# q and k loaded with twelve tokens of one head per partition, and transposed in 64 by 64 pieces

## The chip, the core and the metric

The kernel runs on one core of a Trainium2 chip. The core has five engines that run side by side, each through its own instructions in order: TensorE (PE in the profile; its weight loads are shown apart as PEld), VectorE (DVE), ScalarE (ACT), GpSimd (POOL) and SyncE (SP). Data comes from HBM into SBUF by DMA, through 16 DMA engines that all queues share. TensorE reads SBUF and writes PSUM, and VectorE and ScalarE take results out of PSUM. SBUF and PSUM have 128 partitions each.

The metric is the device time of one execution in microseconds (us). The time before is 165.16 us, the median of three runs (163.99, 165.16 and 166.20).

## The reference

The program is an attention that looks at few chunks of keys, and a soft mixture of experts (MoE) over its result. Sizes: 4 batches, 8 heads, 768 tokens, head dimension 64; chunks of 32 keys, of which 6 are chosen per query; 8 experts with 4 slots each, model width 512, hidden width 1024.

```
k_min, k_max = min and max of k over each chunk of 32 keys
ub     = sum_d max(q * k_min, q * k_max)       # bound of a query's score with a chunk
ub     = where(chunk not after the query's chunk, ub, -1e9)
chosen = the 6 chunks with the largest ub, per query
scores = q @ k.T / sqrt(64), -1e9 where the chunk isn't chosen or the key is later
attn   = softmax(scores) @ v                   # 4 x 8 x 768 x 64

x      = attn as 3072 x 512
logits = x @ phi                               # 3072 x 32
d      = softmax of logits over the tokens;  slot_in = d.T @ x
slot_out[e] = relu(slot_in[e] @ w1[e]) @ w2[e]
out    = softmax of logits over the slots @ slot_out
```

## The kernel before

The attention is worked through in 16 pairs of heads: pair i holds two heads of one batch, and each batch has four pairs. For a product over the head dimension, q and k must lie in SBUF with that dimension on the partitions. The kernel keeps them as `kT` and `qT`, 128 partitions by 768 tokens in bf16: partitions 0 to 63 are the 64 dimensions of the pair's first head, 64 to 127 those of the second.

The path from HBM to `kT` (and to `qT` alike) has three steps.

- `load` (L141 to L147) issues one DMA from GpSimd for one pair and one tensor. It converts from f32 to bf16. In `k_in` (or `q_in`), partition p holds tokens 6p to 6p + 5 of the first head and then the same tokens of the second: two runs per partition, each 6 x 64 f32 values or 1.5 KB in HBM.
- `transposes` (L203 to L213) makes 12 transposing matmuls. For each of the six token places g and each head h, 128 partitions by 64 columns of `k_in` are the stationary operand, and the 128 by 128 identity moves through. The result, 64 dimensions by 128 tokens, goes to the partition half h of the PSUM tile `tr_ps`, at place g. Both heads' pieces thus stand in the same PSUM tile, one above the other.
- `evac_T` (L215 to L222) is one ScalarE copy of `tr_ps` into `kT`, which puts the tokens into their order: token 6p + g is read from place g, column p.

`kT` is then read by VectorE for the chunks' minima and maxima (`kmin`, `kmax`), and by TensorE for the scores. `qT` is split by VectorE into its negative and positive parts (`qsplit`, tile `qpn`), which `ubound` multiplies with the chunks' bounds (tile `ub_ps`). `select` takes the six largest on VectorE, `ns_transposes` brings the choice to the scores' layout, and `scores` (L294 to L313) adds the product of q and k (L301) and the mask of the choice (L311) in PSUM. `expo` takes the exponential on ScalarE (L325), GpSimd masks the blocks on the diagonal (L335), `pv` multiplies with v (L353, tile `at_ps`), and `normalise` divides on VectorE. The result is transposed (`x_transposes`, L375) and goes into the MoE.

The order of work is written out by hand, engine by engine. In step i of the loop over pairs, the scores and exponentials of pair i run in six groups; between them stand the bounds and the choice of pair i + 1, the transposes of pair i + 2, the products with v of pair i - 1, and the normalisation and transposes of pair i - 2. On TensorE, the k transposes follow the bounds (`ubound(i + 1)`) and precede `pv(i - 1, [0, 1, 2])` and the scores of groups 2 and 3; the q transposes follow `pv(i - 1, [3])` and precede the scores of group 4. On ScalarE, the copy to `kT` stands between the exponentials of groups 1 and 2, the copy to `qT` between those of groups 3 and 4. The scores go through two PSUM tiles of two banks each, one bank per head. The tile `tr_ps` shares two one-bank buffers (`p_tp`) with the other small results of TensorE.

Loads are issued from GpSimd, whose instructions run in order with the masks: k and q of pair i + 4 in step i, v of pair i + 2, and one or two of the 16 weight blocks of the experts (1 MB each in SBUF, `w_sb`). The loop starts at step 1. Ahead of it, pairs 0 and 1 are prepared with filler matmuls on TensorE (`warm`, L201) between their transposes, step 0 is written out by itself with the transposes of pair 2, and the loads of pairs 0 to 4 are issued. After the loop come the last pair, the experts, and the output.

Of the kernel before, what the change touches and what calls it, by code (L numbers as in the profile page):

```python
# [11 lines left out]
BF16 = mybir.dt.bfloat16  # L12
# [8 lines left out]
NQT = 6  # L21
P = 128
S = 768
D = 64
# [36 lines left out]
def kernel(  # L61
# [10 lines left out]
    nc = tc.nc  # L72
# [6 lines left out]
    SPE = NS // E  # L79
    NDG, NFG = Dm // P, F // P  # L80
    EARLY = 14
    LAST = NPAIR - 1

    ctx.enter_context(tc.manual_schedule())
# [5 lines left out]
    p_tp = ctx.enter_context(tc.tile_pool(name="p_tp", bufs=2, space=PSUM))  # L90
# [4 lines left out]
    ident = static.tile([P, P], BF16, name="ident")  # L95
# [9 lines left out]
    w1p = w_ctx.enter_context(tc.tile_pool(name="w1p", bufs=1, side="right"))  # L105
    for i in range(EARLY):
        w_sb.append((w1p if i < E else static).tile([P, NDG * F], BF16, name=f"w_sb{i}"))
# [21 lines left out]
    inp = l_ctx.enter_context(tc.tile_pool(name="inp", bufs=3, side="right"))  # L129
# [11 lines left out]
    def load(i, nm):  # L141

        b, j = divmod(i, NPB)
        t = inp.tile([P, 2, NQT * D], BF16, name=nm + "_in", tag=nm + "_in")
        src = {"k": k, "q": q}[nm][b, 2 * j:2 * j + 2]
        nc.gpsimd.dma_start(out=t, in_=src.rearrange("h (p g) d -> p h (g d)", p=P))  # L146
        st[nm, i] = t  # L147

    def load_v(i):
        b, j = divmod(i, NPB)  # L150
        nc.gpsimd.dma_start(  # L151
            out=v_t[i % NV][:, :, :, :D],
            in_=v[b, 2 * j:2 * j + 2].rearrange("h (g p) d -> p h g d", p=P),
        )


    nc.vector.memset(ones_sq, 1.0)
    load(0, "k")
    load(0, "q")
    make_identity(nc, ident)  # L160
    for t in (squad, caus, qgrp, headsel, ns_t[0], ns_t[1], c_pad):
# [6 lines left out]
    for j in range(4):  # L168
# [3 lines left out]
        out=squad, in_=squad, compare_op=ALU.not_equal, fill=NEG, base=0,  # L172
# [3 lines left out]
        out=squad, in_=squad, compare_op=ALU.not_equal, fill=-1.0, base=-NCHUNK,  # L176
        pattern=[[-CH, 2], [-64, 2], [0, NCHUNK]], channel_multiplier=1,
    )
    load(1, "k")
    load(1, "q")  # L180
    nc.gpsimd.affine_select(
        out=qgrp, in_=qgrp, compare_op=ALU.not_equal, fill=1.0, base=0,
# [3 lines left out]
        out=caus[:4], in_=caus[:4], compare_op=ALU.is_ge, fill=NEG, base=0,  # L186
# [15 lines left out]

    def transposes(i, nm):  # L203

        ps = p_tp.tile([P, NQT, P], BF16, name="tr_ps", tag="tp")
        src = st.pop((nm, i))
        for g in range(NQT):
            for h in range(2):
                nc.tensor.matmul(  # L209
                    ps[h * 64:(h + 1) * 64, g, :], lhsT=src[:, h, g * D:(g + 1) * D], rhs=ident,  # L210
                    is_transpose=True,
                )
        st[nm + "ps", i] = ps  # L213

    def evac_T(i, nm):  # L215

        t = tp3.tile([P, S], BF16, name=nm + "T", tag=nm + "T")
        nc.scalar.copy(  # L218
            t.rearrange("d (p g) -> d p g", g=NQT),
            st.pop((nm + "ps", i)).rearrange("d g p -> d p g"),  # L220
        )
        st[nm + "T", i] = t  # L222
# [71 lines left out]
    def scores(i, g):  # L294
        ps = p_sc.tile([P, 2, 512], F32, name="sc_ps", tag="sc")
        kT, qT, nsT = st["kT", i], st["qT", i], st["nsT", i]
        for kg, q0, w, c in (GROUPS_LAST if i == LAST else GROUPS)[g]:
            qs = slice(kg * P + q0, kg * P + q0 + w)
# [19 lines left out]
    def expo(i, g, masked=True):  # L318
        pieces = (GROUPS_LAST if i == LAST else GROUPS)[g]
        w = sum(x[2] for x in pieces)  # L320
        if w == 512:
            e = ep.tile([P, 2, 512], BF16, name="e_sb", tag="e_sb")
        else:
            e = ep3.tile([P, 2, 384], BF16, name="e3_sb", tag="e3_sb")
        nc.scalar.activation(e[:, :, :w], st.pop(("scps", i, g))[:, :, :w], func=ACT.Exp, scale=scale)  # L325

        st["e", i, g] = e
        if masked:
            mask(i, g)

    def mask(i, g):
        e = st["e", i, g]
        for kg, q0, _, c in (GROUPS_LAST if i == LAST else GROUPS)[g]:
            if q0 == 0:
# [5 lines left out]
    def pv(i, ts):  # L340
        if i == LAST and ts[0] == 0:
            st["at", i] = p_tp.tile([P, 2, 3 * (D + 1)], F32, name="at_ps", tag="tp")
        elif i == LAST and ts[0] == 3:
            st["at", i] = p_sc.tile([P, 2, 512], F32, name="at_ps", tag="sc")
        elif ts[0] == 0:
            st["at", i] = p_at.tile([P, 2, 512], F32, name="at_ps", tag="at")
        at, tb = st["at", i], 3 if i == LAST and ts[0] > 2 else 0
        for t in ts:
            for h in range(2):
                o = at[:, h, (t - tb) * (D + 1):(t - tb + 1) * (D + 1)]  # L350
                for kg in range(t + 1):
                    g, c = (BLOCK_LAST if i == LAST else BLOCK)[(kg, t)]
                    nc.tensor.matmul(  # L353
                        o, lhsT=st["e", i, g][:, h, c:c + P], rhs=v_t[i % NV][:, h, kg, :],
                        start=(kg == 0), stop=(kg == t),
                    )
# [163 lines left out]
    def have(i):  # L520
        return 0 <= i < NPAIR
# [10 lines left out]
    def weights(i):  # L532
        nonlocal nw
        for _ in range(wplan.get(i, 0)):
            load_w(nw)
            nw += 1

    warm(9)
    transposes(0, "k")
    evac_T(0, "k")  # L540
    kmin(0)
    kmax(0)
    warm(3)
    transposes(0, "q")
    evac_T(0, "q")
    qsplit(0)
    warm(2)
    transposes(1, "k")
    evac_T(1, "k")
    warm(2)  # L550
    ubound(0)
# [39 lines left out]
    for i in range(1, NPAIR):  # L591
        slots = have(i - 3) and (i - 3) % NPB == NPB - 1
        if i >= EARLY:
            wt = ctx.enter_context(tc.tile_pool(name=f"wt{i}", bufs=1))
# [47 lines left out]
        if have(i + 2):  # L642
            load_v(i + 2)
        if i < EARLY:
            weights(i)
# [77 lines left out]
    def cinv(n):  # L723
# [5 lines left out]
        bc, lhsT=mneg.broadcast_to([NS, P]), rhs=identf[:NS, :NS], start=True, stop=True,  # L729
# [159 lines left out]
    for m in range(1, NM):  # L889
        o_sb = op.tile([P, 2, Dm], F32, name="o_sb", tag="o_sb")  # L890
        for x, scaled in enumerate((scaled_act, scaled_dve)):
            tag = ("sc", "tp", "tp", "sc", "at")[n % 5]
# [38 lines left out]
```

## Time and profile before

| | |
|---|---|
| time, median of three runs | 165.16 us |
| the profiled execution's own time | 164.61 us |
| its span, first to last instruction | 162.9 us |
| TensorE busy | 140.9 us, 86% of the span |
| VectorE busy | 123.3 us, 76% |
| ScalarE busy | 122.3 us, 75% |
| GpSimd busy | 103.2 us, 63% |
| mean granted TensorE clock | 0.953 |
| read from HBM | 52.49 MB |

The profile is that of one execution, and its times count from the start of the span. Matmuls are pipelined: a matmul's shown duration reaches from its start to its end, and the next one starts long before that end, so what a matmul costs is read from the distance between starts. A row of the timeline joins instructions of one line that follow one another; its two numbers are the start of the first and the time to the end of the last. In a group's row, the busy time and the mean duration in ns are followed by the idle time of the engine just before the group's instructions, and by what ended most of it. The chain of waits is followed back from the last instruction: at each step to what released it, or to the instruction before it on its engine.

### The profile page before, as it was taken

How to read it: one execution, taken by the hardware profiler on the slowest of the kernel's cores; microseconds unless marked ns; L12 is line 12 of the kernel's file. 1: busy time of each engine (PE TensorE's matmuls, PEld its weight loads, DVE VectorE, ACT ScalarE, POOL GpSimd, SP SyncE). 2: the span in 40 equal slices, each digit the busy share in tenths (PEclk: the TensorE clock that was granted, in tenths of full speed). 3: DMA queues.
4: the chain of work that ended last, by engine and by line, in shares of the span. 5: the costliest groups of instructions: out<-in, count | busy, mean ns of one | idle time of the engine just before them, and what ended most of it. 6: DMA issues, size and time to landing. Idle time of an engine off the chain costs nothing.

```text
span 162.9 us, 5890 instructions
## 1 busy us (share of the span) xinstructions
PE 140.9 (86%) x2417; PEld 91.6 (56%) x2417; DVE 123.3 (76%) x434; ACT 122.3 (75%) x168; POOL 103.2 (63%) x203
## 2 busy tenths in 40 slices
PE   7796779999999999999999899998989899986600
PEld 2253456767767686676768567676857544442100
DVE  4466989999999999999997999898555632177620
ACT  3758879999999898999989799996986122075520
POOL 6988759989889498978959897859845400000000
PEclk9999999999999999999999999999999959999555
DMA  3999999999999999999999999999999999229996
GB/s 43 149 148 159 208 179 127 173 197 202 202 202 203 202 206 180 207 198 183 214 191 211 197 208 195 212 214 197 210 199 214 215 215 211 59 82 406 404 404 255
DMA packets 40603, 32.92 MB, mean 202 GB/s; under 512 B 26368, under 2 KB 34816, under 8 KB 40576
## 3 DMA queue, kind: packets, MB, share of 16 engines
q0 software_dynamic: 38416, 26.25, 109.2%
q1 hardware_dynamic: 2160, 6.29, 9.9%
q8 instruction: 19, 0.31, 0.7%
q14 instruction: 8, 0.07, 0.1%
HBM read 52.49 MB, written 6.29 MB: 361 GB/s over the span
## 4 chain that ended last, share of the span: by engine, by line
PE 49%; ACT 17%; DVE 11%; DMA 8%; issue 6%; POOL 4%; POOLq 0%; ACTq 0%; DVEq 0%
ACT e_sb L325 11%; PE sc_ps L301 9%; PE at_ps L353 8%; PE sc_ps L311 6%; DMA out_dram<-o_sb 5%; PE tr_ps L209 5%; PE xT_ps L375 4%; ACT qT L218 3%; PE h_ps L790 3%; DMA k_in<-in_k_dram 3%; PE ub_ps L260 2%; PE so_ps L824 2%; DVE x_sb L366 2%; PE ub_ps L253 1%; DVE mx L272 1%
## 5 line engine op out<-in xcount | busy, mean ns | idle before, releaser
L325 ACT ACTIVATE e_sb<-sc_ps 128x1024 bf16<-128x1024 f32 (+1 forms) x96 | 83.2, 917 | 7.8 <-PE sc_ps L311 7.2
L335 POOL TENSOR_SCALAR_AFFINE_SELECT e_sb<-e_sb 128x256 bf16<-128x256 bf16 x96 | 38.5, 418 | 16.1 <-ACT e_sb L325 15.6
L301 PE MATMUL sc_ps<-qT,kT 64*128 64x384 bf16 (+3 forms) x258 | 36.8, 305 | 2.5 <-ACT e_sb L325 1.6
L311 PE MATMUL sc_ps<-nsT,smask 64*128 64x384 bf16 (+2 forms) x294 | 38.1, 284 | 0.1
L353 PE MATMUL at_ps<-v_t,e_sb 128*128 128x65 bf16 x672 | 29.8, 194 | 1.7 <-DVE x_sb L366 1.3
L353 PEld LDWEIGHTS <-e_sb 128*128 128x128 bf16 x672 | 25.6, 98 | 4.0 <-issue 2.6
L301 PEld LDWEIGHTS <-kT 64*128 64x128 bf16 x258 | 13.9, 93 | 10.6 <-issue 5.3
L272 DVE MAX8 mx<-ub_ps 128x8 f32<-128x8 f32 (+1 forms) x192 | 16.8, 162 | 3.7 <-PE ub_ps L260 2.8
L311 PEld LDWEIGHTS <-smask 64*128 64x128 bf16 x294 | 14.9, 94 | 3.9 <-issue 0.6
L151 POOL DMA_DIRECT2D v_t<-in_v_dram x16 | 16.6, 1038 | 0.6 <-PE ns_ps L283 0.5
L227 DVE TENSOR_REDUCE mm<-kT 128x24 bf16<-128x768 bf16 x16 | 15.1, 944 | 2.2 <-ACT kT L218 2.2
L366 DVE TENSOR_TENSOR x_sb<-at_ps,inv 128x768 bf16<-128x768 f32 (+1 forms) x17 | 15.5, 910 | 0.6
L233 DVE TENSOR_REDUCE mm<-kT 128x24 bf16<-128x768 bf16 x16 | 15.1, 943 | 0.0
L218 ACT COPY qT<-tr_ps 128x768 bf16<-128x768 bf16 x16 | 12.8, 800 | 2.3 <-PE tr_ps L209 2.3
L218 ACT COPY kT<-tr_ps 128x768 bf16<-128x768 bf16 x16 | 12.8, 802 | 1.0 <-PE tr_ps L209 1.0
L146 POOL DMA_DIRECT2D k_in<-in_k_dram x16 | 11.8, 735 | 1.1 <-POOLq L915 0.8
L146 POOL DMA_DIRECT2D q_in<-in_q_dram x16 | 11.5, 716 | 0.0
L139 POOL DMA_DIRECT2D w_sb<-in_moe_w_dram x16 | 11.4, 712 | 0.0
L386 DVE COPY xT_sb<-xT_ps 128x768 bf16<-128x768 bf16 (+1 forms) x15 | 8.0, 537 | 2.6 <-PE xT_ps L375 2.6
L894 PE MATMUL o_ps<-so_all,cT_all 128*128 128x512 bf16 x22 | 7.5, 428 | 2.5 <-ACT o_sb L856 2.2
L247 DVE TENSOR_SCALAR qpn<-qT 128x768 bf16<-128x768 bf16 x15 | 9.2, 610 | 0.0
L209 PE MATMUL tr_ps<-ident,k_in 128*64 128x128 bf16 x192 | 8.4, 223 | 0.6 <-DMA k_in<-in_k_dram 0.5
(137 smaller groups left out, 206.3 us busy)
## 6 DMA issues: line engine op xcount, KB each, us to landing
w_sb<-in_moe_w_dram POOLq DMA_DIRECT2D x16, 1024.0 KB, 12.6
out_dram<-o_sb SPq DMA_DIRECT2D x10, 512.0 KB, 4.9
k_in<-in_k_dram POOLq DMA_DIRECT2D x16, 192.0 KB, 6.3
q_in<-in_q_dram POOLq DMA_DIRECT2D x16, 192.0 KB, 6.9
v_t<-in_v_dram POOLq DMA_DIRECT2D x16, 192.0 KB, 7.7
out_dram<-o_sb SPq DMA_DIRECT2D x2, 256.0 KB, 4.1
out_dram<-first SPq DMA_DIRECT2D x2, 128.0 KB, 2.0
out_dram<-first SPq DMA_DIRECT2D x1, 256.0 KB, 2.1
```

What stands on the lines that cost most here:

```text
L146: nc.gpsimd.dma_start(out=t, in_=src.rearrange("h (p g) d -> p h (g d)", p=P))
L151: nc.gpsimd.dma_start(out=v_t[i % NV][:, :, :, :D], in_=v[b, 2 * j:2 * j + 2].rearrange("h (g p) d -> p h g d", p=P),)
L209: nc.tensor.matmul(ps[h * 64:(h + 1) * 64, g, :], lhsT=src[:, h, g * D:(g + 1) * D], rhs=ident, is_transpose=True,)
L218: nc.scalar.copy(t.rearrange("d (p g) -> d p g", g=NQT), st.pop((nm + "ps", i)).rearrange("d g p -> d p g"),)
L227: nc.vector.tensor_reduce(mm[:, 0, 0, :], kT, axis=AX.X, op=ALU.min)
L272: nc.vector.max(mx[:, a, :], ub[:, a, :max(8, 4 * t + 4)])
L301: nc.tensor.matmul(ps[:, h, c:c + w], lhsT=kT[r, kg * P:(kg + 1) * P], rhs=qT[r, qs], start=True, stop=False,)
L311: nc.tensor.matmul(ps[:, h, c + (f - t0) * P:c + (l - t0) * P], lhsT=smask[r, x, kg].rearrange("p a b -> p (a b)"), rhs=nsT[r, (f - x * NJ ...
L325: nc.scalar.activation(e[:, :, :w], st.pop(("scps", i, g))[:, :, :w], func=ACT.Exp, scale=scale)
L335: nc.gpsimd.affine_select(out=e[:, :, c:c + P], in_=e[:, :, c:c + P], compare_op=ALU.is_ge, fill=0.0, base=0, pattern=[[0, 2], [1, P]], ch ...
L353: nc.tensor.matmul(o, lhsT=st["e", i, g][:, h, c:c + P], rhs=v_t[i % NV][:, h, kg, :], start=(kg == 0), stop=(kg == t),)
L366: nc.vector.tensor_tensor(st["x", b][:, t0:t1, 2 * j:2 * j + 2, :].rearrange("p t h d -> p h t d"), at[:, :, :, :D], inv.broadcast_to([P, ...
```

## The change

`load` gives each partition twelve consecutive tokens of one head: partition 64h + p holds tokens 12p to 12p + 11 of head h, one run of 12 x 64 f32 values or 3 KB in HBM. `transposes` works on pieces of 64 partitions by 64 columns, with the matching 64 by 64 part of the identity: 24 matmuls for a pair and a tensor, whose results fill the same 768 columns of `tr_ps` as 12 places of 64. The pieces of the first head use partitions 0 to 63 of SBUF and of PSUM, those of the second 64 to 127. `evac_T` reads token 12p + g from place g, column p. `kT` and `qT` hold the same as before.

```diff
+    NT2 = 2 * NQT
...
-        t = inp.tile([P, 2, NQT * D], BF16, name=nm + "_in", tag=nm + "_in")
+        t = inp.tile([P, NT2 * D], BF16, name=nm + "_in", tag=nm + "_in")
         src = {"k": k, "q": q}[nm][b, 2 * j:2 * j + 2]
-        nc.gpsimd.dma_start(out=t, in_=src.rearrange("h (p g) d -> p h (g d)", p=P))
+        nc.gpsimd.dma_start(out=t, in_=src.rearrange("h (p g) d -> (h p) (g d)", g=NT2))
...
-        ps = p_tp.tile([P, NQT, P], BF16, name="tr_ps", tag="tp")
+        ps = p_tp.tile([P, NT2, 64], BF16, name="tr_ps", tag="tp")
         src = st.pop((nm, i))
-        for g in range(NQT):
+        for g in range(NT2):
             for h in range(2):
+                r = slice(h * 64, (h + 1) * 64)
                 nc.tensor.matmul(
-                    ps[h * 64:(h + 1) * 64, g, :], lhsT=src[:, h, g * D:(g + 1) * D], rhs=ident,
-                    is_transpose=True,
+                    ps[r, g, :], lhsT=src[r, g * D:(g + 1) * D], rhs=ident[r, r], is_transpose=True,
                 )
...
-            t.rearrange("d (p g) -> d p g", g=NQT),
+            t.rearrange("d (p g) -> d p g", g=NT2),
```

## The prediction

> **What bounds the kernel now.** I read the totals by line first, to see what the transposes are worth at all.
>
> ```profile
> PEclk9999999999999999999999999999999959999555
> ...
> L218 ACT COPY kT<-tr_ps 128x768 bf16<-128x768 bf16 x16 | 12.8, 802 | 1.0 <-PE tr_ps L209 1.0
> ...
> L209 PE MATMUL tr_ps<-ident,k_in 128*64 128x128 bf16 x192 | 8.4, 223 | 0.6 <-DMA k_in<-in_k_dram 0.5
> ```
>
> The k transposes keep TensorE busy for 8.4 us, those of q for as long, and the granted clock is full while they run: every slice up to the 32nd shows a 9. Whether they set the end is read from one steady pair of heads: first TensorE alone, then ScalarE alone.
>
> ```profile
> 48.02 0.53 PE L209 MATMUL tr_ps<-ident,k_in 128*64 128x128 bf16 x12
> 48.48 0.55 PE L353 MATMUL at_ps<-v_t,e_sb 128*128 128x65 bf16 x12
> 48.96 0.34 PE L301 MATMUL sc_ps<-qT,kT 64*128 64x384 bf16 x2
> 49.14 0.33 PE L311 MATMUL sc_ps<-nsT,smask 64*128 64x384 bf16 x2
> 49.30 0.33 PE L301 MATMUL sc_ps<-qT,kT 64*128 64x384 bf16 x2
> 49.46 0.33 PE L311 MATMUL sc_ps<-nsT,smask 64*128 64x384 bf16 x2
> 49.72 0.51 PE L375 MATMUL xT_ps<-ident,x_sb 128*128 128x128 bf16 x6
> 50.07 0.41 PE L353 MATMUL at_ps<-v_t,e_sb 128*128 128x65 bf16 x8
> 50.41 0.53 PE L209 MATMUL tr_ps<-ident,q_in 128*64 128x128 bf16 x12
> ```
> ```profile
> 48.72 0.81 ACT L218 COPY kT<-tr_ps 128x768 bf16<-128x768 bf16 x1
> 49.56 1.51 ACT L325 ACTIVATE e_sb<-sc_ps 128x768 bf16<-128x768 f32 x2
> 50.98 0.80 ACT L218 COPY qT<-tr_ps 128x768 bf16<-128x768 bf16 x1
> 51.67 1.03 ACT L325 ACTIVATE e_sb<-sc_ps 128x1024 bf16<-128x1024 f32 x1
> ```
>
> ScalarE is nearly gapless, yet TensorE leads it here. The copy of qT starts at 50.98 and the next exponential already at 51.67, 0.69 later. The copy of kT starts at 48.72, and the exponential after it only at 49.56, 0.84 later: 0.15 us of waiting, for scores that end at 49.14 + 0.33 = 49.47 and stand behind the k transposes and the products at L353. So a longer k transpose is paid in full. For q the last piece ends at 50.41 + 0.53 = 50.94, and the exponentials leave ScalarE free at about 49.56 + 1.51 - 0.10 = 50.97: the slack is 0.03 us. The chain of waits says the same:
>
> ```profile
> 48.09 0.46 PE tr_ps L209 x12
> ...
> 50.48 0.46 PE tr_ps L209 x12
> ...
> 52.78 0.59 PE lg_ps L395 x24
> ```
>
> Both sets lie on it. Fourteen pairs of heads (2 to 15) are transposed between the scores of earlier pairs, so 28 sets count; those of pairs 0 and 1 stand in the start, between filler matmuls.
>
> **What a set costs now.** A set of 12 takes 48.48 - 48.02 = 0.46 us, start to the start of what follows. To split it I cut the same spot finer:
>
> ```profile
> 48.02 0.14 PEld L209 LDWEIGHTS <-k_in 128*64 128x64 bf16 x4
> 48.02 0.25 PE L209 MATMUL tr_ps<-ident,k_in 128*64 128x128 bf16 x2
> ```
> ```profile
> 48.02 0.30 PE L209 MATMUL tr_ps<-ident,k_in 128*64 128x128 bf16 x4
> ```
>
> Two pieces together last 0.25 us, hardly more than one (0.22 to 0.24): the two heads, which write upper and lower halves of PSUM, run side by side. Four last 0.30, so the second couple starts about 0.08 after the first; twelve last 0.53, so the sixth starts about 0.53 - 0.22 = 0.31 after it, and a couple costs (0.31 - 0.08) / 4 = 0.057. That is the price of 128 columns: at L375 six such matmuls, one by one, last 0.51, (0.51 - 0.22) / 5 = 0.058 each. The weight loads are covered. Price follows columns: couples of 384 wide follow one another every 49.30 - 49.14 = 0.16, which is 0.053 per 128. The rest, 0.46 - 0.31 = 0.15, is the last couple's own 0.055 and a change-over of about 0.10 to the next array shape.
>
> **The change, part by part.** *Transposes.* 24 pieces of 64 rows by 64 columns in place of 12 of 128 by 128, 12 couples in place of 6. If couples still run side by side and cost by width, one costs 0.027 to 0.029. The second then starts 0.08 - 0.028 = 0.052 after the first, ten more make 0.29, and the end is 0.15 - 0.028 = 0.12: 0.46 to 0.47 against 0.46. I take +0.01 per set, times 28: **+0.3 us**. Half the columns, twice the couples: nothing is won or lost. The shapes before and after the set stay others than its own, so the change-overs stay two.
>
> No row shows a 64 by 64 piece, so bounds are needed. Below, 0.0: a tile cannot pass 64 columns faster than 384 go by at L301. Above, pieces that go singly at a full transposing matmul's price, L375: 23 x 0.058 + 0.15 = 1.48, +1.0 per set or +28 us. I take the couples' price, because L209 itself shows couples writing one PSUM tile (768 bf16 values, 1.5 KB a partition) in the same instant, and L301 shows upper and lower rows at work together.
>
> That tile is also where a rule speaks against the change. The Trainium skill, TensorEngine Tiling (Array Packing), Restrictions and Gotchas, says that different row tiles cannot access one PSUM bank at the same time. The two scores at L301 go to different banks, so no run here shows row tiles sharing one. By that rule the pieces would go singly, the second rival below; without it the sum stays +0.3.
>
> *Copies out of PSUM.* Same 128x768, each run of the inner loop 12 long rather than 6. The nearest row with no stride at all is the one copy that ScalarE makes at L386:
>
> ```profile
> 125.34 0.80 ACT L386 COPY xT_sb<-xT_ps 128x768 bf16<-128x768 bf16 x1 [0.52 <-PE xT_ps L375]
> ```
>
> 0.80 like L218, so stride costs nothing: 0.
>
> *Loads.* Same bytes in half the packets.
>
> ```profile
> L151 POOL DMA_DIRECT2D v_t<-in_v_dram x16 | 16.6, 1038 | 0.6 <-PE ns_ps L283 0.5
> ...
> L146 POOL DMA_DIRECT2D k_in<-in_k_dram x16 | 11.8, 735 | 1.1 <-POOLq L915 0.8
> ```
> ```profile
> k_in<-in_k_dram POOLq DMA_DIRECT2D x4, 192.0 KB, 10.1
> ```
> ```profile
> 43.05 0.72 POOL L146 DMA_DIRECT2D k_in<-in_k_dram  x1
> ```
> ```profile
> 55.20 0.46 PE tr_ps L209 x12
> ```
>
> Issuing: v with 1536 pieces costs 1038 ns, k with 256 costs 735, so 128 fewer save about 0.03, 1 us of GpSimd over 32 loads; GpSimd is not on the chain in the steady pairs, so I count 0. Landing: 10.1 us in the stretch from 27 to 53 us, while k issued at 43.05 is used at 55.20, 12.1 later. A faster load gains nothing there; one slower by over 2 us would stall TensorE. Fewer, longer runs give no reason for that.
>
> In the start a load can matter:
>
> ```profile
> 4.01 4.16 DMA k_in<-in_k_dram
> ```
> ```profile
> 4.32 1.47 ACT L192 COPY smask<-schunk 128x1536 bf16<-128x1536 bf16 x1 [2.23 <-DVE schunk L191]
> ...
> 8.55 0.35 DVE L243 TENSOR_SCALAR qpn<-qT 128x768 bf16<-128x768 bf16 x1
> ...
> 9.12 0.29 PE L253 MATMUL ub_ps<-caus,qgrp 128*128 128x288 bf16 x1
> ```
>
> The second k load takes 4.16 us and TensorE waits for it. But the first bound product, at 9.12, needs qpn, ready at 8.55 + 0.35 = 8.90, the end of a VectorE chain from the kT copy, which stands behind the mask copy on ScalarE, not behind a load. So at most 9.12 - 8.90 = 0.2 comes back, however fast the loads. I take **-0.2**.
>
> *Sum:* +0.3 - 0.2 = +0.1. The profiled execution took 164.61 (span 162.9 and 1.7 around it) and would take 164.7. The median shown is 165.16, so the forecast is **165.2 us**: no change that a measurement can tell (about 2%, 3.3 us).
>
> **Rivals.** *A fixed price per piece (slower).* At L395, matmuls 32 wide follow every 0.59 / 24 = 0.025 us, though a price by width would be 0.014. If that were a price of each instruction, couple or not, a set has 24 x 0.025 = 0.60, plus 0.12 of end: 0.72, +0.26. For k all of it counts, for q 0.23: 0.49 x 14 = 6.9. In the start I count 0.3 for the four sets less the 0.2 of the loads: 165.2 + 7.0 = **172.2**. It decides as soon as a couple costs over 0.029. Against it: the couple's two pieces start within 0.01 of each other at L209, so 0.025 looks like the price of one tile being used again, and 64 columns already take 0.027. The Trainium skill, TensorEngine Tiling (Array Packing), Instruction Overhead, speaks of about 60 cycles per matmul, so that one column costs what 60 do. The row at L395 agrees; whether tiles share it, neither says.
>
> *One piece at a time (slower).* If the pieces of a couple exclude each other, 24 x 0.029 + 0.12 = 0.82, +0.36 per set: 28 x 0.36 = 10.1 less the 0.4 of slack for q, and 0.2 in the start: 165.2 + 9.9 = **175.1**. For it, only the bank rule; against it the couples at L209.
>
> *A faster start.* If loads shorten and the 0.2 is all that was late, 164.7 with transposes at no cost. To be faster by 2%, each of the 28 sets would have to lose 0.12, which 64 columns at the rate of L301 do not allow.
>
> *The halving is not there.* If each 3 KB run were still moved as two packets, the 0.2 of the start is not won: 165.5.
>
> **How the numbers follow.** Forecast with its neighbours (faster start, no halving): 0.60. Fixed price per piece, or part of it: 0.25. One at a time or worse: 0.10. Something that I do not see on the fast side: 0.05. The range goes from 163.5, the faster start's 164.7 less the 1.2 by which the lowest run of before (163.99) lies under its median, to 172.8, which takes in the fixed price; the last two, 0.15, are left out. The likeliest case alone would be 164.2 to 166.3. Within 2%: 0.60; slower: 0.35; faster: 0.05.
>
> **What would show it.** In the changed profile, 24 pieces of 64*64 should last about 0.54 us in one row of the timeline, and the next matmuls start 0.47 after them; 0.77 to 0.80 means a fixed price, 0.89 one at a time. The wait of the exponential after kT should stay near 0.15. Packets of k and q should be half as many, 4096 fewer in the software queue. The first bound product should stand near 8.95. The forecast is wrong if the row of 24 is long, or if TensorE waits for k or q after 20 us.

## The result, and the profile after

The changed kernel takes 167.87 us (median of 20 runs, 165.75 to 170.64) against 164.98 for the kernel before (20 runs, 163.00 to 166.20). The ratio is 1.0143, with a 95% interval of 1.0113 to 1.0174: slower by 1.4%, or about 2.4 us, and so within the 2% that the forecast called no change. The ratios in this document are taken over the runs that lie within 1.5% of the fastest of their kernel (here 13 of 20 on either side), so they can differ from the quotient of the medians. The 167.87 lies inside the range of 163.5 to 172.8, 2.7 us above the 165.2 that was named. The profiled execution took 167.35 us, with a span of 165.6, against 164.61 and 162.9.

The page of the changed kernel, its totals, clock, queues and the groups of the change:

```profile
PE 141.2 (85%) x2801; PEld 94.6 (57%) x2801; DVE 121.4 (73%) x434; ACT 123.0 (74%) x168; POOL 98.7 (60%) x203
...
PEclk9999999999999999999999999999999999999955
...
q0 software_dynamic: 34320, 26.25, 105.0%
...
q8 instruction: 22, 0.36, 0.8%
...
L147 POOL DMA_DIRECT2D k_in<-in_k_dram x16 | 9.2, 578 | 1.1 <-POOLq L916 0.8
L211 PE MATMUL tr_ps<-ident,k_in 64*64 64x64 bf16 x384 | 9.5, 197 | 0.0
...
L147 POOL DMA_DIRECT2D q_in<-in_q_dram x16 | 8.7, 544 | 0.7 <-PE tr_ps L211 0.7
```

The lines of the page before that answer to them, as far as they were not shown:

```profile
PE 140.9 (86%) x2417; PEld 91.6 (56%) x2417; DVE 123.3 (76%) x434; ACT 122.3 (75%) x168; POOL 103.2 (63%) x203
...
q0 software_dynamic: 38416, 26.25, 109.2%
...
q8 instruction: 19, 0.31, 0.7%
...
L146 POOL DMA_DIRECT2D q_in<-in_q_dram x16 | 11.5, 716 | 0.0
```

Three readings. TensorE's busy time hardly moved, and its clock is full up to the last two slices, so neither more work nor the throttle is the loss. The software queue has 38416 - 34320 = 4096 packets fewer, as the change says. TensorE has 384 more matmuls and as many more weight loads, 768 instructions, and the queue named "instruction" has three more packets. I had passed over that queue.

A steady pair shows that the transposes do what the forecast said. First TensorE, then ScalarE, in the pair whose transposes start at 41.65:

```profile
41.65 0.57 PE L211 MATMUL tr_ps<-ident,k_in 64*64 64x64 bf16 x24
42.15 0.55 PE L354 MATMUL at_ps<-v_t,e_sb 128*128 128x65 bf16 x12
...
43.73 0.41 PE L354 MATMUL at_ps<-v_t,e_sb 128*128 128x65 bf16 x8
44.08 0.56 PE L211 MATMUL tr_ps<-ident,q_in 64*64 64x64 bf16 x24
44.57 0.28 PE L302 MATMUL sc_ps<-qT,kT 64*128 64x256 bf16 x2
```
```profile
44.08 0.22 PE L211 MATMUL tr_ps<-ident,q_in 64*64 64x64 bf16 x2
```
```profile
42.34 0.81 ACT L219 COPY kT<-tr_ps 128x768 bf16<-128x768 bf16 x1
43.23 1.51 ACT L326 ACTIVATE e_sb<-sc_ps 128x768 bf16<-128x768 f32 x2
```

A set of 24 lasts 0.56 to 0.57, and the next matmuls start 44.57 - 44.08 = 0.49 to 0.50 after its start. The starts in the trace give 0.497 against 0.458 before, in all sets that wait for nothing. The two pieces of a couple last 0.22 together, no more than one alone: they run side by side. The exponential after kT starts 43.23 - 42.34 = 0.89 after the copy, where it was 0.84: its wait grew by 0.05, as the set did. A steady pair lasts 6.585 us, 0.08 more than the 6.505 before, twice 0.04.

So the longer sets make 28 x 0.04 = 1.1 us. The rest of the loss is no steady one. Against the kernel before, the q transposes start 0.17 us later at 44 us, 1.24 at 59, 2.59 at 81 and 2.82 at 110.65, in steps, and this is one of them:

```profile
72.47 0.34 PE L302 MATMUL sc_ps<-qT,kT 64*128 64x384 bf16 x2
73.37 0.34 PE L312 MATMUL sc_ps<-nsT,smask 64*128 64x384 bf16 x2 [0.56 <-issue]
73.54 0.33 PE L302 MATMUL sc_ps<-qT,kT 64*128 64x384 bf16 x2
```
```profile
73.81 1.51 ACT L326 ACTIVATE e_sb<-sc_ps 128x768 bf16<-128x768 f32 x2 [0.81 <-PE sc_ps L312]
```

The matmuls at L312 follow those at L302 by 0.90 instead of 0.17, and the trace names no releaser: "issue" is time in which the engine waits for nothing that the profile shows. ScalarE then waits 0.81 us. The operands were there, and what was missing was the instruction. The transfers of the stretch from 71.0 to 71.1 us have the answer:

```profile
q0 software_dynamic: 10, 0.02, 89.0%
q8 instruction: 1, 0.02, 60.9%
```

One packet of code starts here, at 71.00 in the trace, 2.37 us before TensorE goes on. 22 packets carry 0.36 MB, 16 KB each, or 256 instructions of 64 bytes; 22 x 256 = 5632, and TensorE has 2 x 2801 = 5602. Its waits without a releaser all stand at one place of the count: over matmuls and weight loads 74 to 82 instructions before a multiple of 256, and with the 28 instructions of its sequencer counted too (semaphores and the like), 63 or 64 before it every time. Worked out from the starts in the trace, for each such boundary of the changed kernel from 46 us on: when the packet started, when TensorE crossed the boundary, how long after the packet that is, and how far apart the two matmuls at the boundary started (0.01 to 0.17 where nothing waits):

```
packet   crossed   packet to crossing   step at the boundary
 46.66     49.14        2.48                 0.53
 52.80     55.30        2.50                 0.55
 58.94     61.33        2.39                 0.42
 64.28     67.18        2.90                 no wait
 71.00     73.37        2.37                 0.89
 75.83     79.12        3.29                 no wait
 82.24     84.76        2.52                 0.36
 88.64     91.06        2.42                 0.32
 93.66     96.94        3.28                 no wait
 99.55    102.31        2.76                 no wait
105.99    108.47        2.48                 0.16
112.28    114.76        2.48                 1.29 (other waits in it)
```

Wherever there is a wait, it ends 2.37 to 2.52 us after the packet began, and where there is none the packet began 2.76 us or more ahead. The kernel before has 2.84 us or more at every boundary of its loop, and no such wait. The account that fits is a race of two periods. In the table a packet starts 2.5 to 3.9 us after TensorE has crossed the boundary before, while the DMA engines are full, and its code can be used some 2.4 us later: 4.9 to 6.3 in all. A block of 256 instructions lasted 256/244 x 6.505 = 6.8 us in a steady pair before, and 256/292 x 6.585 = 5.8 us now.

The Trainium skill, Runtime: NRT & Kernel Launch, Instruction fetch mechanics, states that code is refilled in blocks of 16 KiB, 256 instructions, over a DMA queue of the sequencer's own, and that crossing into a new block is mostly hidden. The sizes agree with the rows above. That it is hidden holds for the kernel before and not for the changed one, which is held up by as much as 0.89 - 0.17 = 0.72 us at a crossing.

### The profile page after: what moved, and what is told of

It reads as the page before. It is cut to its first block, busy times and chain, and to the rows that moved or that the text cites. A ratio compares the mean times of both kernels' runs of the same rounds, so it can differ in the third digit from the quotient of the medians.

```text
span 165.6 us, 6658 instructions
## 1 busy us (share of the span) xinstructions
PE 141.2 (85%) x2801; PEld 94.6 (57%) x2801; DVE 121.4 (73%) x434; ACT 123.0 (74%) x168; POOL 98.7 (60%) x203
## 3 DMA queue, kind: packets, MB, share of 16 engines
q0 software_dynamic: 34320, 26.25, 105.0%
## 4 chain that ended last, share of the span: by engine, by line
PE 49%; ACT 19%; DVE 12%; issue 8%; DMA 5%; POOL 2%; ACTq 0%; DVEq 0%
ACT e_sb L326 12%; PE sc_ps L302 8%; PE at_ps L354 7%; PE sc_ps L312 6%; DMA out_dram<-o_sb 5%; PE tr_ps L211 5%; PE xT_ps L376 4%; ACT qT L219 4%; PE warm_ps L202 3%; PE ub_ps L261 2%; PE h_ps L791 2%; PE so_ps L825 2%; DVE x_sb L367 2%; PE ub_ps L254 1%; DVE mx L273 1%
## 5 line engine op out<-in xcount | busy, mean ns | idle before, releaser
L302 PE MATMUL sc_ps<-qT,kT 64*128 64x384 bf16 (+3 forms) x258 | 37.0, 305 | 4.0 <-ACT e_sb L326 1.6
L312 PE MATMUL sc_ps<-nsT,smask 64*128 64x384 bf16 (+2 forms) x294 | 38.4, 284 | 0.8 <-issue 0.6
L302 PEld LDWEIGHTS <-kT 64*128 64x128 bf16 x258 | 14.0, 93 | 10.9 <-issue 6.4
L312 PEld LDWEIGHTS <-smask 64*128 64x128 bf16 x294 | 15.0, 94 | 5.3 <-issue 2.1
L147 POOL DMA_DIRECT2D k_in<-in_k_dram x16 | 9.2, 578 | 1.1 <-POOLq L916 0.8
L211 PE MATMUL tr_ps<-ident,k_in 64*64 64x64 bf16 x384 | 9.5, 197 | 0.0
L895 PE MATMUL o_ps<-so_all,cT_all 128*128 128x512 bf16 x22 | 6.5, 377 | 3.3 <-ACT o_sb L857 3.1
L147 POOL DMA_DIRECT2D q_in<-in_q_dram x16 | 8.7, 544 | 0.7 <-PE tr_ps L211 0.7
L211 PE MATMUL tr_ps<-ident,q_in 64*64 64x64 bf16 x384 | 9.0, 194 | 0.0
```

The lines of the kernel that those rows point to most:

```text
L147: nc.gpsimd.dma_start(out=t, in_=src.rearrange("h (p g) d -> (h p) (g d)", g=NT2))
L211: nc.tensor.matmul(ps[r, g, :], lhsT=src[r, g * D:(g + 1) * D], rhs=ident[r, r], is_transpose=True,)
L302: nc.tensor.matmul(ps[:, h, c:c + w], lhsT=kT[r, kg * P:(kg + 1) * P], rhs=qT[r, qs], start=True, stop=False,)
L312: nc.tensor.matmul(ps[:, h, c + (f - t0) * P:c + (l - t0) * P], lhsT=smask[r, x, kg].rearrange("p a b -> p (a b)"), rhs=nsT[r, (f - x * NJ ...
```

## The experiments

Two questions: which half of the change costs what, and are the waits really for code.

**The loads alone.** Twelve old transposes read the new layout, so the tokens come out permuted.

```diff
-        t = inp.tile([P, 2, NQT * D], BF16, name=nm + "_in", tag=nm + "_in")
+        t = inp.tile([P, 2 * NQT * D], BF16, name=nm + "_in", tag=nm + "_in")
-        nc.gpsimd.dma_start(out=t, in_=src.rearrange("h (p g) d -> p h (g d)", p=P))
+        nc.gpsimd.dma_start(out=t, in_=src.rearrange("h (p g) d -> (h p) (g d)", g=2 * NQT))
...
-                    ps[h * 64:(h + 1) * 64, g, :], lhsT=src[:, h, g * D:(g + 1) * D], rhs=ident,
+                    ps[h * 64:(h + 1) * 64, g, :], lhsT=src[:, (2 * g + h) * D:(2 * g + h + 1) * D], rhs=ident,
```

> The new loads (runs of 3 KB) with the twelve old 128 by 128 transposes. The partitions then hold other tokens than the transposes take them for, so the result is not the reference's; the work is the same. Theory A (the time comes from TensorE's instructions: 0.04 us more per set of transposes, and waits at the ends of blocks of 256 instructions, whose code comes late over the busy DMA engines): within 0.3% of before, 164.5 to 165.4, a plain pair of heads every 6.50 us. Theory B (the longer runs land at other times and the waits in the loop are waits for data): at least half of the 2.4 us, 166.2 or more.

Measured: 163.44 us (12 runs) against 165.01, ratio 0.9914 (0.9879 to 0.9949). The loads win 1.4 us by the ratio, which I had put at next to nothing. The profile shows over a third of it at one place. Before, VectorE and then GpSimd around the split of q for pair 3:

```profile
20.25 0.91 DVE L243 TENSOR_SCALAR qpn<-qT 128x768 bf16<-128x768 bf16 x1
21.09 0.55 DVE L247 TENSOR_SCALAR qpn<-qT 128x768 bf16<-128x768 bf16 x1
```
```profile
19.23 0.72 POOL L146 DMA_DIRECT2D q_in<-in_q_dram  x1
19.94 1.04 POOL L151 DMA_DIRECT2D v_t<-in_v_dram  x1
```

The same two views with the new loads:

```profile
20.27 0.57 DVE L243 TENSOR_SCALAR qpn<-qT 128x768 bf16<-128x768 bf16 x1
20.75 0.34 DVE L247 TENSOR_SCALAR qpn<-qT 128x768 bf16<-128x768 bf16 x1
```
```profile
19.07 0.55 POOL L146 DMA_DIRECT2D q_in<-in_q_dram  x1
19.61 1.04 POOL L151 DMA_DIRECT2D v_t<-in_v_dram  x1
```

The same VectorE operation on the same shape takes 0.34 us or up to 0.91. Not every one beside an issue is long: the split at 8.55 in the kernel before took 0.35 while GpSimd issued q from 8.43 to 9.15. But each of the long ones here ends just after an instruction of GpSimd that ran beside it: the one of 0.91 ends at 21.16 and the issue of v at 20.98, the one of 0.57 at 20.84 and the issue at 20.65. In the traces of the kernel before and of this run, every split of over 0.36 us ends 0.16 to 0.22 after such an instruction, a DMA's issue or a mask. The rows read as a hold until about then. With k and q issued 0.16 to 0.17 us faster each, v is issued 0.33 earlier, the two splits end at 21.09 instead of 21.64, and the k transposes of pair 3 start at 21.53 instead of 22.07: 0.54 us, which stay won up to the last transposes. Over the whole kernel the 31 splits take 17.0 us before and 13.9 here; in most pairs that is slack. At the last q transposes 0.76 us are won, at the end of the profiled execution 1.3. In the last 0.5 no operation stands out, and I do not put it down to the loads.

**The pieces alone.** The old loads and 24 pieces of 64 by 64; the tokens come out permuted here too.

```diff
-        for g in range(NQT):
+        for g in range(NT2):
...
+                r = slice(h * 64, (h + 1) * 64)
-                    ps[h * 64:(h + 1) * 64, g, :], lhsT=src[:, h, g * D:(g + 1) * D], rhs=ident,
-                    is_transpose=True,
+                    ps[r, g, :], lhsT=src[r, g // NQT, (g % NQT) * D:(g % NQT + 1) * D], rhs=ident[r, r], is_transpose=True,
```

> The old loads (runs of 1.5 KB) with the 24 transposes of 64 by 64. The partitions hold other tokens than the transposes take them for, so the result is not the reference's; the work is the same. Theory A: all of the loss, ratio 1.011 to 1.017, a plain pair every 6.58 us, and waits of 0.2 to 0.8 us on TensorE once per 256 of its instructions in several places after 45 us. Theory B: below 166.0. Theory C (only the sets' own length counts, 28 x 0.04 = 1.1 us): 166.1, ratio 1.007, no such waits.

Measured: 168.95 us (6 runs), ratio 1.0259 (1.0207 to 1.0311). That is above the 1.011 to 1.017 that I had named for late code. By the ratios the loads give -1.4 us and the pieces +4.3, together +2.9, where the change has +2.4; the intervals leave room for that much. The kernel waits at the same instruction as the changed one. From its timeline, and then from that of the changed kernel:

```profile
55.32 0.23 PE L302 MATMUL sc_ps<-qT,kT 64*128 64x128 bf16 x1
55.88 0.21 PE L302 MATMUL sc_ps<-qT,kT 64*128 64x128 bf16 x1 [0.34 <-issue]
```
```profile
54.75 0.23 PE L302 MATMUL sc_ps<-qT,kT 64*128 64x128 bf16 x1
55.30 0.21 PE L302 MATMUL sc_ps<-qT,kT 64*128 64x128 bf16 x1 [0.33 <-issue]
```

Two matmuls that otherwise start within 0.01 us of each other stand 0.55 apart in both kernels. They are the two heads of one score product, which read the same two tiles, so no wait for data would part them. What lies between them is the place of the count at which the table has all its waits.

**The weights late.** In the changed kernel, 14 of the 16 weight blocks are loaded in step 14, so that the DMA engines are not full before.

```diff
-    wplan = {1: 1, 2: 1, 3: 1, 4: 1, 6: 1, 8: 1, 9: 1, 10: 1, 11: 2, 12: 1, 13: 2, 14: 1, 15: 1}
+    wplan = {14: 14, 15: 1}
```

> The changed kernel, with the loads of weight blocks 1 to 14 moved from the steps 1 to 14 to step 14, so that the DMA engines are idle much of the loop; the end then waits for the weights and its time says nothing. What counts is when the q set of the last pair starts (107.8 us before, 110.6 changed). Theory A: no waits at the ends of blocks, plain pairs still 6.58, and that set starts at 108.3 to 109.2. Theory C: the waits of the loop were chance or data and stay: 110 or later.

Measured: 211.97 us in one run, with the wait for the weights at its end. The last q transposes start at 108.16, against 110.65 in the changed kernel and 107.83 before; I had named 108.3 to 109.2, without the loads' gain. At the instruction that waited at 73.37 nothing waits now:

```profile
71.09 0.34 PE L302 MATMUL sc_ps<-qT,kT 64*128 64x384 bf16 x2
71.26 0.33 PE L312 MATMUL sc_ps<-nsT,smask 64*128 64x384 bf16 x2
```

From 48 us to the last transposes the packets of code start within about 1 us of the crossing before, not 2.5 to 3.9 after it, and come 4.7 us or more ahead of need. The sum closes: 107.83 + 1.1 for the longer sets - 0.8 for the loads = 108.1. With the same instructions, the waits vanish with the traffic. Laid side by side matmul by matmul, the changed kernel falls behind this run at seven of the boundaries in the table, by 0.13 to 0.72 us and 2.8 in all; between boundaries it loses over 0.1 us at no place after 7 us. With the 0.3 us that it is behind from the start, and 0.6 caught up on the way, that is the whole distance of 2.49.

**k alone, q alone.** Loads and pieces of the change for one of the two tensors, the kernel before for the other; the one for k is shown.

```diff
+        if nm == "k":
+            nc.gpsimd.dma_start(out=t, in_=src.rearrange("h (p g) d -> (h p) (g d)", g=NT2))
+        else:
+            nc.gpsimd.dma_start(
+                out=t.rearrange("p (h x) -> p h x", h=2), in_=src.rearrange("h (p g) d -> p h (g d)", p=P))
...
+        n = NT2 if nm == "k" else NQT
```

> k alone by the change (3 KB loads, 24 pieces), q as before; the result is the reference's. Theory (code comes late): TensorE has 268 instructions in a plain pair, so a block of 256 lasts 256/268 x 6.55 = 6.26 us, where the changed kernel has 5.8 and the kernel before 6.8. In the changed kernel a block came 4.9 to 6.7 us after the one before it was begun, so here waits of more than 0.45 us should be gone and at most 0.8 us of them is left in all. 14 sets at +0.04 are +0.55, half of the loads' gain of 1.5 is -0.75: 165.0 + 0.55 - 0.75 + 0 to 0.8 = 164.8 to 165.6. Rival (a loss that goes with each piece): half of the changed kernel's +2.9, 166.4.

> The mirror of the run with k alone: q by the change, k as before; the result is the reference's. Theory (code comes late): the same 268 instructions in a plain pair, 164.8 to 165.6. Rival (a loss that goes with each piece): 166.4. Should the two runs differ by over 0.7 us, then it is the place of the pieces that counts (for k they are on the path in full, for q there was 0.03 us of slack), and neither theory has it.

Measured: 164.82 us for k, ratio 0.9977 (0.9939 to 1.0015), and 164.91 for q, 0.9999 (0.9959 to 1.0038), 12 runs each. Both are inside the band that the late code gives and below the 166.4 of a loss that goes with each piece. One wait of note is left with k alone, at 64.95, and none with q alone:

```profile
64.95 0.34 PE L313 MATMUL sc_ps<-qT,kT 64*128 64x384 bf16 x2 [0.25 <-issue]
```

Half the added instructions cost not half the loss but almost none of it: a threshold, as two periods that race would give (a block of 256 lasts 6.26 us in these two kernels, against the 4.9 to 6.3 that the code needs).

**The loads with their time given back to GpSimd.** If the loads win because GpSimd is free earlier, work of the same length behind each load must take the gain away. A memset of 128x64 on GpSimd stands behind each k and q load.

```diff
         nc.gpsimd.dma_start(out=t, in_=src.rearrange("h (p g) d -> (h p) (g d)", g=2 * NQT))
+        nc.gpsimd.memset(spare, 0.0)
```

> The 3 KB loads with the old transposes (tokens come out permuted, as in the first run), and behind each k and q load a memset of 128x64 on GpSimd, which should last about 0.16 us: what the shorter issue had saved. Theory (the loads' gain is GpSimd's issue time): the gain goes, 164.6 to 165.3, 0.997 to 1.002 of the kernel before. Rival (the gain is the landing in half as many packets): it stays, 163.2 to 163.7, 0.989 to 0.992.

Measured: 163.94 us (10 runs), ratio 0.9916 (0.9879 to 0.9953). The memsets last 0.174 us each, 5.6 in all, yet the gain stays: my theory falls as a whole. At pair 3 it holds in part. The splits of q, and the issue of v beside them:

```profile
19.99 0.74 DVE L245 TENSOR_SCALAR qpn<-qT 128x768 bf16<-128x768 bf16 x1
20.66 0.55 DVE L249 TENSOR_SCALAR qpn<-qT 128x768 bf16<-128x768 bf16 x1
```
```profile
19.42 0.18 POOL L148 MEMSET spare<- 128x64 bf16 x1
19.51 1.04 POOL L153 DMA_DIRECT2D v_t<-in_v_dram  x1
```

They are held again. The k transposes of pair 3 start at 21.64, 0.43 earlier than in the kernel before, but 0.26 of that was already there at the q transposes ahead of them (18.20 against 18.46), so of the 0.54 us only 0.17 are left at this place. In later pairs the splits are as short as with the loads alone: 13.2 us for all 31. So the length of the issue decides at one pair, and what else the loads win, about 1 us, is not explained by it. The rival, landing in half as many packets, fits the time, but no wait in these profiles shows landing on the path, and so the rest stays open. That execution, one of the longer ones of this kernel (165.58), also shows a wait for code with the instruction count of the kernel before:

```profile
36.97 0.36 PE L211 MATMUL tr_ps<-ident,q_in 128*64 128x128 bf16 x6
37.79 0.36 PE L211 MATMUL tr_ps<-ident,q_in 128*64 128x128 bf16 x6 [0.46 <-issue]
```

Its packet began at 35.58, 2.21 us earlier and 5.1 us after the crossing before, where the changed kernel has 3.9 at most. So a packet can start later still, and even 244 instructions in a pair are not far from the threshold.

**Instructions without work.** NoOps on TensorE were to add count and nothing else. The first run has 8 behind each group of scores, 48 in a pair, in the kernel before; the second has the same with the weights late.

```diff
+        for n in range(8 if i < NPAIR - 2 else 0):
+            nc.tensor.nop(hint='x', nofuse=True)
```

> The kernel before with 672 empty instructions on TensorE, eight after each of the six groups of scores of pairs 0 to 13, which is as many as the change adds in its 28 sets; loads and transposes as before. Theory A: sets stay at 0.46 and a plain pair at 6.50, but waits of 0.2 to 0.8 us appear about every 256 instructions, 1 to 2 us in all: 166.0 to 167.2. Theory C: 165.0, nothing but what an empty instruction itself costs, which would show as a longer plain pair, the same in each.

> The kernel before with the 672 NoOps on TensorE, and weight blocks 1 to 14 all loaded in step 14; the whole time says nothing then, the loop up to the transposes of pair 15 does. Theory (code comes late behind a full DMA): no waits of TensorE at block ends, the last q transposes start at 107.8 to 108.5 as in the kernel before (107.83), and the NoOps cost nothing by themselves. Rival (NoOps or their number cost time on TensorE): the last q transposes stand past 112, with losses that grow by a constant amount per pair.

Measured: 177.88 us (6 runs), ratio 1.0659 (1.0577 to 1.0741), or 10.9 us: five times the most that I had expected. The profiled execution took 177.76, the fastest 174.65. Its profile shows steps like this one:

```profile
51.17 0.36 PE L283 MATMUL ns_ps<-ident,ns_t 128*128 128x128 bf16 x3 [1.90 <-issue]
```

Laid beside the kernel before matmul by matmul, it loses about 8.2 us in six such steps between 36 and 91 us, of 0.46 to 2.0 us each. Four of them stand at the same place of the count as the waits above, 63 or 64 instructions before a multiple of 256 with NoOps and sequencer counted, and the other two a few NoOps further on. With the weights late (211.69 us in one run), the last q transposes stand at 109.21, 1.38 after those of the kernel before, where with the weights in their places they stand at 120.52, 12.69 after. The direction is that of late code, and 11.3 of the 12.7 us go with the traffic. Two things missed. The 1.38 is more than the up to 0.7 that I had allowed, so the NoOps are not free. And why code comes so much later beside NoOps than beside pieces is open.

Two more runs put the same number at the places of the pieces, 24 behind each set, once with the new loads and once with the old.

```diff
+        for n in range(24 if i >= 2 else 0):
+            nc.tensor.nop(hint="x", nofuse=True)
         st[nm + "ps", i] = ps
```

> The 3 KB loads with the 12 old transposes (tokens come out permuted, as in the first run), and 24 NoOps on TensorE behind each set of pairs 2 to 15: as many instructions in a pair as the changed kernel has, at the same places, but no more work. Theory (code comes late): up to the last q transposes the changed kernel loses 2.8 us to the kernel before, the loads alone win 0.8 and the longer sets cost 28 x 0.04 = 1.1, so 2.5 us are waits for code; they come back here: 163.4 + 2.5, 165.5 to 166.8, with waits of TensorE at block ends from 48 us on. Rival (it is the pieces, not their number of instructions): as the loads alone, 163.2 to 164.0, no waits.

> The kernel before with 24 NoOps on TensorE behind each set of pairs 2 to 15: the count of the earlier run with 672 NoOps, which lost 12.9 us, but in 28 places rather than 84. Theory (code comes late, as in the run with the pieces alone, which has the same count, the old loads and 3.9 us of loss, 1.1 of it longer sets): 165.0 + 2.8, 167 to 169. Rival (old loads and NoOps lose far more than pieces do, wherever they stand): 174 to 180.

Measured: 189.35 us (6 runs) and 190.73 (4 runs), ratios 1.1531 (1.1464 to 1.1597) and 1.1585 (1.1520 to 1.1651). Neither theory had that. With the old loads, the timeline around a q set:

```profile
51.50 0.53 PE L209 MATMUL tr_ps<-ident,q_in 128*64 128x128 bf16 x12
52.97 0.28 PE L303 MATMUL sc_ps<-qT,kT 64*128 64x256 bf16 x2 [0.95 <-ACT qT L220]
```

The step from the set to the next matmuls is 1.47 us instead of 0.46, 1.0 us more for 24 NoOps. In the trace NoOps in a row start 0.071 us apart, which makes 1.7 us for 24; the first of these starts at 51.31, ahead of the set's matmuls, so part of them runs beside other work. The releaser named, a copy of ScalarE, is only what came last. In these kernels a pair lasts about 8.5 us, so its blocks are longer than before and code is not late: the two runs say nothing on the question that they were made for. They agree with the loads' gain, 190.73 - 189.35 = 1.4 us, though the times of the two overlap.

**The change where there is room for it.** The change for pairs 0 to 5 alone, ahead of the stretch in which code came late.

```diff
+        if i < 6:
+            nc.gpsimd.dma_start(out=t, in_=src.rearrange("h (p g) d -> (h p) (g d)", g=NT2))
+        else:
...
+        n = NT2 if i < 6 else NQT
```

> The change for pairs 0 to 5 alone, loads and pieces, the kernel before for pairs 6 to 15; the result is the reference's. Theory (code comes late only while the weight blocks fill the DMA engines, from 48 us on in the changed kernel; the loads win 0.5 us at pair 3, where the split of q waits for the issue of v): no waits for code, 8 sets in the loop at +0.04 are +0.3, -0.5 at pair 3, the last q transposes 0.0 to 0.5 us earlier than in the kernel before, 164.5 to 165.2. Rival (the loss goes with each piece): 12 of 32 sets, +1.1 of the 2.9 us, 166.1.

Measured: 164.14 us (12 runs) against 164.80, ratio 0.9964 (0.9929 to 0.9998). No wait without a releaser is left in its loop, and the last q transposes are 0.31 us earlier than in the profile before, inside the 0.0 to 0.5 given. The time itself is a little under the 164.5 to 165.2 named. Of the versions here that compute all of the reference it is the fastest, 0.4% under the kernel before, which the interval only just tells from nothing.

## Why the prediction was right, and where it was not

- **No change by over 2%: right**, with about +2.4 us where +0.1 was summed. The sum missed one whole term and sized two others wrongly. That the time stayed under 2% is in part luck: the pieces alone cost 4.3 us, or 2.6%, and what brings it back is a gain of the loads that the sum did not have.
- **Couples side by side: right.** Neither a fixed price per piece (0.77 to 0.80 in one row) nor one piece at a time (0.89) came; the row lasts 0.56 to 0.57 where 0.54 was named. The rule of the Trainium skill on row tiles that share a PSUM bank (TensorEngine Tiling (Array Packing), Restrictions and Gotchas) did not act here: two pieces that write one tile of 1.5 KB a partition last 0.22 together.
- **"One costs 0.027 to 0.029": too low.** In the trace the second couple starts 0.052 after the first, as summed, but each of the next ten 0.032 after the one before it, and the end is 0.125. That makes 0.497, or +0.04 per set, not +0.01: 1.1 us, not 0.3. The step scaled the price by columns from pieces twice and six times as wide; a small part of it does not scale. Of the fixed-price rival this much was true.
- **Copies at nothing: right**, 0.799 us for qT and 0.802 for kT, against 0.800 and 0.802.
- **Code: the missing term.** I counted the 12 more couples as time of the array and not as 768 more instructions that have to be brought by DMA in a kernel whose DMA engines are full. Waits for code cost about 2.5 us up to the last transposes: 2.82 lost, less 1.1 for the sets, plus 0.8 that the loads win. Undone by late weights and by half the pieces, and found at the same instruction in two kernels, this is shown. What sets the time from a crossing to the start of the next packet was not measured by itself; the runs show only that it is long with full DMA engines.
- **"128 fewer save about 0.03": wrong.** A load takes 578 and 544 ns where it took 735 and 716; the saving is 0.16 to 0.17. I had drawn a line through v, with 1536 pieces, and k, and a line does not hold there.
- **"GpSimd is not on the chain in the steady pairs, so I count 0": wrong at pair 3**, where VectorE is held until GpSimd has issued v, and 0.5 us come back. The loads alone win 1.4 us; about 1 us of it stays unexplained.
- **First bound product near 8.95, and 0.2 us won in the start: the row was misread.** The row at 9.12 reads `caus` and `qgrp` and not `qpn`; it starts at 9.02 now. The first row that reads `qpn` is the one behind it, L260 before and L261 now, and it came 0.47 later instead of earlier:

```profile
9.24 0.46 PE L260 MATMUL ub_ps<-bd,qpn 128*128 128x48 bf16 x12
```
```profile
9.02 0.29 PE L254 MATMUL ub_ps<-caus,qgrp 128*128 128x288 bf16 x1
9.71 0.47 PE L261 MATMUL ub_ps<-bd,qpn 128*128 128x48 bf16 x12 [0.41 <-DVE qpn L244]
```

Its operand came late for the reason found at pair 3: the split is held until 0.18 us after the issue of v, which lasts from 8.43 to 9.47. With the loads alone the same split starts at 8.82, takes 0.36, and the product starts at 9.23, so even there nothing is won against 9.24. The held split of the changed kernel:

```profile
8.83 0.82 DVE L244 TENSOR_SCALAR qpn<-qT 128x768 bf16<-128x768 bf16 x1
```

- **Packets halved: right**, 4096 fewer; and TensorE waits for neither k nor q after 20 us.

## What to carry to other kernels

Count the instructions of the busiest engine as data: divide 256 by its instructions per step of the loop, times the length of the step, and compare that with the time that a code packet needs in that stretch (here mostly 4.9 to 6.3 us with full DMA engines). Splitting work into more and smaller instructions can be nearly free on the engine and still cost time at such block ends. Where an operation of VectorE has two lengths on the same shape, look at what GpSimd does beside it, and at which of the two ends just after the other.

## What the runs showed of the hardware

- TensorE's code comes in packets of 16 KB, one per 256 instructions. Waits ended 2.37 to 2.52 us after the packet's start in the changed kernel. The packet started 2.5 to 3.9 us after the crossing before with full DMA engines (5.1 once, in the run with memsets), and within about 1 us with the weights late.
- Couples of 64 by 64 transposing pieces follow one another every 0.032 us, those of 128 by 64 every 0.056.
- NoOps in a row on TensorE start 0.071 us apart; 24 behind a set put the next matmuls 1.0 us later. Spread in groups of 8, 672 of them cost 1.4 us by the last transposes where code was not late.
- The split of 128x768 on VectorE takes 0.34 us, or up to 0.91 when it is held; in the kernel before and with the loads alone a held one ends 0.16 to 0.22 us after the DMA issue or the mask of GpSimd that ran beside it. Some with an issue beside them throughout are not held (0.35 at 8.55). The Trainium skill, SBUF — State Buffer, Who interferes with whom, says that VectorE in its two-port modes and GpSimd exclude each other for whole instructions, and that the order of issue decides who waits. The rows agree that one is held. At pair 3 the long split ends at 21.16, 0.18 after the issue of v does, which is less than the split's own 0.34, so it was not held for the whole of it.
